# A fused attention and FFN kernel: one run of small products per head pair, and two banks each for FFN1 and attention

## The chip, the cores and the metric

One Trainium2 chip, of which the kernel uses one core. The metric is the device time of the program in microseconds. It runs once per measurement; three runs of the kernel before are shown, and a profile of one execution of it.

## The reference

Eight batches, eight heads, 576 tokens of 64 elements. Linear attention without softmax, a root-mean-square norm over each head, a low-rank mixing over the tokens (rank 32), and an FFN of 512 to 2048 to 512:

```python
kv = np.einsum('bhsd,bhse->bhde', k, v)
out = np.einsum('bhsd,bhde->bhse', q, kv)
rms = np.sqrt(np.mean(out * out, axis=-1, keepdims=True) + 1e-06)
x = (out / rms * g_norm)            # heads side by side: (batch, 576, 512)
u = x + ((x.transpose(0, 2, 1) @ U) @ V).transpose(0, 2, 1)
y = u + np.maximum(u @ w_ch1, 0.0) @ w_ch2
```

## The kernel before, in words

**The FFN.** The 4608 tokens are cut in nine blocks of 512. Each product of the FFN is made of three, with both operands split into a high and a low part: high by high, high by low, low by high. Blocks 0 to 2 (`j` in the main loop) go one by one: for each of the 16 slices `f` of the hidden width, `ffn1` (L518 to L520, 12 matmuls of 128x512 into the one bank `h`), the ReLU (`hh` on ACT in L530, `hl` on DVE in L535), and `ffn2` of the slice before (L542, 12 matmuls into four banks `y`). One slice is thus 24 matmuls of 128x512, and a quarter of it is 6. The other six blocks go two by two in three stages (`q`), by a scheme with seven products in place of eight (`first_unit` L705, `second_unit` L807, `end_unit` L757), whose combined weights are made in blocks 0 to 2, stored to DRAM and read back as `wt`. A unit of a stage is 6 matmuls of 128x512, 112 units a stage.

**Attention.** It is done by pairs (b, p): batch b, and two heads side by side in 128 columns. A pair needs these steps, and only the first three and the last use TensorE (PE), each in matmuls that are small beside those of the FFN:

- `kv`: k^T v, ten matmuls of 64 columns (L298, 20 rows in a trace, since a matmul of this type has two), copied by ACT into the diagonal 64x64 blocks of `kvb` (L175);
- `out`: q by kv. For b under 5 five matmuls of 128 columns by the block-diagonal `kvb` (four in L335, one in L337, 10 rows); for b from 5 on 20 matmuls in 64x64 quarters of the array, each head into a bank of its own (L330, 40 rows);
- the norm: for b under 5 ACT squares out of PSUM (L353, L354) and DVE multiplies out of PSUM (L391, L393); for b from 5 on ACT copies both banks out first (L346), squares in SBUF (L349), and DVE multiplies in SBUF (L389). Between them lie a sum (L374) and six small steps on DVE and ACT;
- `turn`: a transpose on DVE (L410) and five DMAs on SyncE's queue (SP) through DRAM into `ut32` (L413, L415);
- `t`: x^T U, six matmuls (four in L421, two in L424, 12 rows), then `t4`, seven small steps on ACT and DVE (L434 to L440);
- `mix`: t4 by V, one or two matmuls of up to 448 columns in two parts (L497), added by DVE to `ut32` or to the stage's input `x32` (L504), and for b up to 2 split into high and low.

**What sets the order.** In the stages PE's order is written by hand: the steps of pair p of batch b stand at `STARTS` plus `PARTS` units; the same holds in block 2 (`STARTS2`, `PARTS2`, in quarters of a slice). In blocks 0 and 1 the steps are put at half slices (`STEPS0`, `STEPS`), and a scheduler orders PE's instructions. ACT, DVE, GpSimd (POOL) and SP are ordered by the scheduler everywhere after the first 30 us; within an engine the order is kept on the chip. The first 30 us are written out (`ORDER0`).

**Banks.** PSUM has eight. In blocks 0 to 2: four for `y`, one for `h`, three that go round (`pp`) for every attention step. In the stages: two each for `z`, `x` and `y` (all called `yy` in rows), one `h` and one `big`; attention uses these last two.

Of the kernel before, what the change touches and what calls it, by code (L numbers as in the profile page):

```python
# [10 lines left out]
F32 = mybir.dt.float32  # L11
F32R = mybir.dt.float32r
# [11 lines left out]
NT = 5  # L24
# [11 lines left out]
QUAD = 5  # L36
NEARLY = 1
STEPS = dict(kv=1, out=2, t=5, mix=7, gap=5)
STEPS0 = dict(kv=6, out=7, t=11, mix=12, gap=4)
# [20 lines left out]
uvA uvD u4h vsh vsl kv0 kvb0 v4g out0 sq0 kv1 red0 ta0 hf0 rc0 kvb1 nw0 w1A out1 mul0 w1D0 kv2 sq1 w1D1 red1 w1B  # L60
tx0 kvb2 w1D2 ta1 hf1 out2 rc1 t4c0 nw1 w1H t4s0 kv3 mul1 w2A sq2 w2D0 tx1 cA red2 kvb3 w2D1 ta2 out3 lw1 lw2 lw3 hf2
# [28 lines left out]
def build(ctx: ExitStack, tc: tile.TileContext, kv_in, kvt0_in, kvt_in, q_in, uv_in, g_in, w_in, out):  # L90
# [5 lines left out]
    sc = ctx.enter_context(tc.tile_pool(name="sc", bufs=1))  # L96
    dec = ctx.enter_context(tc.tile_pool(name="dec", bufs=2))
# [4 lines left out]
    ps_p = first_y.enter_context(tc.tile_pool(name="ps_p", bufs=3, space=bass.MemoryType.PSUM))  # L102
# [10 lines left out]
    st = const.tile([P, 4, BLK], F32, name="st")  # L113
    kvb = [const.tile([P, P], F32, name=f"kvb{i}") for i in range(2)]
# [198 lines left out]
    def out_step(b, p):  # L313
        out_product(b, p)
        squares(b, p)

    def out_product(b, p):
# [16 lines left out]
        for i in range(4):
            nc.tensor.matmul(big[:, i * P:(i + 1) * P], lhsT=qt[:, TAIL + i * P:TAIL + (i + 1) * P], rhs=kb, start=True, stop=True)  # L335
# [962 lines left out]
```

## Time and profile before

| | |
|---|---|
| median of 3 runs | 850.45 us (850.35, 850.45, 852.01) |
| the profiled execution | 846.0 us, of which its span is 844.0 |
| PE busy in the span | 830.6 us, 98% |
| DVE, ACT busy | 584.4 us (69%), 435.7 us (52%) |
| granted TensorE clock, mean | 0.998 |
| DMA, mean rate over the span | 235 GB/s |

A row of the timeline has the start in us, the time in us from the first start to the last end, engine, line, operation, tiles (out<-in), the shapes and the number of instructions merged in it. Ends of matmuls are modelled, and a matmul overlaps the next, so distances here are taken from start to start. A row of waits has who waited for whom, the total in us, the number of waits and the longest. A row of windows has, for each engine, the busy time and the number of instructions, then the clock granted to PE, the busy share of the DMA engines and GB/s. A row of lines has the busy time in us, the mean of one in ns, and the idle time before them.

### The profile page before, as it was taken

What the parts mean: (1) busy time and instruction counts of PE and PEld (TensorE: products, weight loads), DVE (VectorE), ACT (ScalarE), POOL (GpSimd) and SP (SyncE); (2) the same over time, 40 slices, a digit from 0 to 9 for tenths busy, and PEclk for the clock granted to TensorE, in tenths of its full rate; (3) what the DMA queues carried; (4) which work ended last, traced back from release to release, by engine and by line L of the source; (5) the groups of instructions that cost most, each with busy time, mean ns of one, the idle gap of its engine ahead of it and who ended that gap; (6) DMA issues with size and microseconds to landing.
All of it is one profiled execution on the core that took longest, in us unless ns stands there. A gap on an engine that the chain in (4) does not pass through costs nothing.

```text
span 844.0 us, 13330 instructions
## 1 busy us (share of the span) xinstructions
PE 830.6 (98%) x4986; PEld 674.7 (80%) x4986; DVE 584.4 (69%) x1031; ACT 435.7 (52%) x795; POOL 80.8 (10%) x158
## 2 busy tenths in 40 slices
PE   7999999999999999999999999999999999999998
PEld 6778878888878787877777788777888888888887
DVE  5999975876776767567775679657836953572466
ACT  5978752433333435456645664656436724553462
POOL 2002232453400221000000000000000000000000
PEclk9999999999999999999999999999999999999999
DMA  9984765787796777366777767786555585555554
GB/s 346 415 348 139 227 222 192 236 275 241 246 291 220 266 237 271 130 239 229 257 249 266 228 237 261 239 278 234 186 200 200 178 285 189 198 197 200 200 196 153
DMA packets 66352, 198.31 MB, mean 235 GB/s; under 512 B 8176, under 2 KB 27376, under 8 KB 55536
## 3 DMA queue, kind: packets, MB, share of 16 engines
q1 hardware_dynamic: 57184, 167.97, 57.9%
q0 software_dynamic: 8960, 29.37, 10.0%
q8 instruction: 39, 0.64, 0.3%
q14 instruction: 25, 0.20, 0.1%
q10 hardware_dynamic: 144, 0.13, 0.0%
HBM read 146.84 MB, written 50.59 MB: 234 GB/s over the span
## 4 chain that ended last, share of the span: by engine, by line
PE 84%; DVE 6%; DMA 6%; ACT 2%; issue 1%; SPq 1%; POOL 0%; DVEq 0%; ACTq 0%
PE yy L705 27%; PE yy L807 25%; PE y L542 12%; PE h L518 4%; PE h L519 4%; PE h L520 4%; PE ya L757 2%; DMA raw<-w_in 1%; PE pp L335 1%; PE h L298 1%; PE pp L298 1%; DMA wd<-dec 1%; DMA w2raw<-w_in 1%; DVE dec L158 1%; PE h L330 1%
## 5 line engine op out<-in xcount | busy, mean ns | idle before, releaser
L705 PE MATMUL yy<-uc,wt 128*128 128x512 f32 x1008 | 237.0, 392 | 0.0
L705 PEld LDWEIGHTS yy<-uc,wt 128*128 128x128 f32 x1008 | 187.1, 188 | 39.7
L542 PE MATMUL y<-hh,ws 128*128 128x512 f32 x336 | 113.8, 400 | 1.7 <-ACT hh L530 1.7
L807 PE MATMUL yy<-dec,wt 128*128 128x512 f32 x468 | 114.7, 392 | 0.3 <-DVE dec L696 0.3
L807 PE MATMUL yy<-hh,wt 128*128 128x512 f32 x312 | 104.9, 393 | 0.0
L807 PEld LDWEIGHTS yy<-dec,wt 128*128 128x128 f32 x468 | 86.9, 188 | 18.9 <-DVE dec L696 0.7
L696 DVE TENSOR_TENSOR dec<-hk,dec 128x512 fp32r<-128x512 f32 x72 | 48.8, 685 | 39.5 <-ACT dec L735 39.2
L696 DVE TENSOR_TENSOR hl<-hk,hh 128x512 fp32r<-128x512 f32 x72 | 48.3, 686 | 39.6 <-ACT hh L735 39.4
L542 PEld LDWEIGHTS y<-hh,ws 128*128 128x128 f32 x336 | 61.7, 188 | 15.3 <-ACT hh L530 2.8
L807 PEld LDWEIGHTS yy<-hh,wt 128*128 128x128 f32 x312 | 58.6, 188 | 12.8
L518 PE MATMUL h<-ut,ws 128*128 128x512 f32 x168 | 67.3, 400 | 1.4 <-DVE hl L535 1.4
L519 PE MATMUL h<-ut,ws 128*128 128x512 f32 x168 | 65.6, 391 | 0.0
L542 PE MATMUL y<-hl,ws 128*128 128x512 f32 x168 | 65.6, 390 | 0.0
L520 PE MATMUL h<-ut,ws 128*128 128x512 f32 x168 | 65.5, 390 | 0.0
L807 PE MATMUL yy<-hl,wt 128*128 128x512 f32 x156 | 60.8, 390 | 0.0
L735 ACT CAST dec<-hk 128x512 fp32r<-128x512 f32 x72 | 44.2, 620 | 30.1 <-PE yy L807 14.4
L735 ACT CAST hh<-hk 128x512 fp32r<-128x512 f32 x72 | 44.2, 621 | 28.8 <-PE yy L807 24.9
L530 ACT ACTIVATE hh<-h 128x512 fp32r<-128x512 f32 x48 | 28.6, 596 | 50.7 <-PE h L520 50.5
L693 ACT COPY sp<-yy 128x1024 f32<-128x1024 f32 x35 | 35.5, 1014 | 34.5 <-PE yy L705 27.5
L535 DVE SCALAR_TENSOR_TENSOR hl<-h,hh 128x512 fp32r<-128x512 f32 x48 | 32.8, 682 | 19.6 <-ACT hh L530 19.1
L718 ACT ACTIVATE hk<-hk 128x1024 f32<-128x1024 f32 x24 | 25.4, 1060 | 33.0 <-DVE hk L717 32.8
L518 PEld LDWEIGHTS h<-ut,ws 128*128 128x128 f32 x168 | 31.5, 188 | 9.7 <-DVE hl L535 2.5
(238 smaller groups left out, 1342.2 us busy)
## 6 DMA issues: line engine op xcount, KB each, us to landing
wt<-wd SPq DMA_DIRECT2D x84, 1024.0 KB, 4.9
kv_sb<-kv_in SPq DMA_DIRECT2D x29, 512.0 KB, 5.2
raw<-w_in SPq DMA_DIRECT2D x14, 1023.6 KB, 14.8
wd<-dec POOLq DMA_DIRECT2D x44, 256.0 KB, 5.1
wd<-ws POOLq DMA_DIRECT2D x42, 256.0 KB, 4.4
q_sb<-q_in SPq DMA_DIRECT2D x29, 288.0 KB, 4.4
ut<-xd SPq DMA_DIRECT2D x28, 288.0 KB, 3.4
out<-x SPq DMA_DIRECT2D x23, 256.0 KB, 2.9
```

The lines of the kernel that those rows point to most:

```text
L518: nc.tensor.matmul(h, lhsT=w1s[f][0][:, d, :], rhs=uh[d], start=(n == 0), stop=False)
L519: nc.tensor.matmul(h, lhsT=w1s[f][0][:, d, :], rhs=ul[d], start=False, stop=False)
L520: nc.tensor.matmul(h, lhsT=w1s[f][1][:, d, :], rhs=uh[d], start=False, stop=(n == ND - 1))
L530: last["relu"] = nc.scalar.activation(out=last["hh"], in_=h, func=AF.Relu)
L535: last["low"] = nc.vector.scalar_tensor_tensor(out=hl, in0=h, scalar=0.0, in1=last["hh"].bitcast(F32), op0=ALU.max, op1=ALU.subtract)
L542: nc.tensor.matmul(acc, lhsT=w2s[f][w][:, c, :], rhs=h[:, cols], start=(f == 0 and w == 0 and h is hh), stop=(f == NF - 1 and w == 1))
L693: last["unit"] = nc.scalar.copy(out=pair_bank("P6") if name == "P1" else spare(name), in_=acc)
L696: return nc.vector.tensor_tensor(out=out, in0=a, in1=b, op=ALU.subtract)
L705: nc.tensor.matmul(acc[:, i], lhsT=w[:, ws_, e * P:(e + 1) * P], rhs=u[:, e, us], start=name in ("P1", "P5") and e == 0 and k == 0, stop=e ...
L718: last["unit"] = nc.scalar.activation(out=to, in_=to if other else acc, func=AF.Relu)
L735: last["unit"] = nc.scalar.copy(out=hh, in_=src)
L807: nc.tensor.matmul(acc[:, c], lhsT=w[:, ws_, c * P:(c + 1) * P], rhs=h, start=name in ("P1", "P5") and kk == 0 and i == 0, stop=kk == KEEP ...
```

## The change

All attention of pair `now` is gathered into `run(before, now, after)`: in one go PE does `t` of the pair before, `kv` of the pair after, and `out` of this pair. The three share two banks: `t` goes into columns 320 to 447 of the second, `kv` into the last 64 of the first (of the second for odd pairs of batch 1), the two heads of `out` into columns 0 to 319 of both. `out` is done in 64x64 quarters for all pairs, and after the first 30 us always copied out by ACT first. A table `RUNS` says where each run stands, `MIXES` where the mixes do, in quarters of a slice in the blocks and in units in the stages. In the blocks the eight banks are now: four `y`, one `h`, one `two` (FFN1 takes `h` for odd slices and `two` for even ones), two `pp`. PE's order is written by hand from the main loop on. `t4` has three buffers in place of one, `turn` follows the norm at once except for three pairs. In the first 30 us 13 matmuls of 128x128 by zeros (`wa3 wb3 wc4 wd3`) are added on PE, and a memset of `kvb` goes from DVE to POOL.

```diff
-QUAD = 5
-STEPS = dict(kv=1, out=2, t=5, mix=7, gap=5)
-STEPS0 = dict(kv=6, out=7, t=11, mix=12, gap=4)
-STARTS = {5: (0, 11, 22, 33), 6: (44, 55, 67, 78), 7: (3, 14, 25, 36)}
-PARTS2 = dict(kv=0, out=4, turn=8, t=13, mix0=17, mix1=18)
-PARTS = dict(kv=0, out=5, turn=9, t=14, mix0=19, mix1=21)
+RUNS = [((1, 0), (0, 20)), ((1, 1), (0, 28)), ((1, 2), (0, 37)), ((1, 3), (0, 45)), ((2, 0), (0, 54)),
...
+        ((6, 3), (3, 72)), ((7, 0), (3, 84)), ((7, 1), (4, 7)), ((7, 2), (4, 18)), ((7, 3), (4, 29)), (None, (4, 40))]
+MIXES = {(1, 0): ((0, 26),), (1, 1): ((0, 43),), (1, 2): ((0, 51),), (1, 3): ((0, 60),),
...
-uvA uvD u4h vsh vsl kv0 kvb0 v4g out0 sq0 kv1 red0 ta0 hf0 rc0 kvb1 nw0 w1A out1 mul0 w1D0 kv2 sq1 w1D1 red1 w1B
+uvA uvD u4h vsh vsl kv0 wa3 kvb0 v4g out0 wb3 sq0 kv1 wc4 red0 ta0 hf0 rc0 kvb1 nw0 w1A out1 mul0 w1D0 kv2 sq1 w1D1 red1 w1B
...
+def banks():
+    if "big" in second_y:
+        return ps_h.tile([P, 512], F32, name="h"), second_y["big"].tile([P, 512], F32, name="big")
+    return bank(), bank()
...
-        if b >= QUAD:
-            heads = [kv_bank_of(b), big]
-        for i in range(4):
-            nc.tensor.matmul(big[:, i * P:(i + 1) * P], lhsT=qt[:, TAIL + i * P:TAIL + (i + 1) * P], rhs=kb, start=True, stop=True)
+        for i in range(NT):
+            at = TAIL + i * P if i < 4 else 0
+            for half in (0, D):
+                for h, lo in enumerate((0, D)):
+                    nc.tensor.matmul(heads[h][half:half + D, i * D:(i + 1) * D], lhsT=qt[lo:lo + D, at + half:at + half + D],
+                                     rhs=kb[lo:lo + D, lo:lo + D], start=True, stop=True)
...
-        t4 = sc.tile([P, P], F32R, name="t4")
+        t4 = four.tile([P, P], F32R, name="t4")
...
+    def run(before, now, after):
+        one, two = banks()
+        if before:
+            t_product(*before, two[:, NT * D:NT * D + P])
+        if after:
+            kv = (two if after[0] < NATIVE and after[1] % 2 else one)[:, BLK - D:]
+            kv_product(*after, kv)
+        if now:
+            out_product(*now, (one, two))
+        if before:
+            t4_step(*before)
+        if after:
+            kv_move(*after, kv)
+            following(load_kv, *after)
+        if now:
+            squares(*now)
+            stats_step(*now)
+            mul_step(*now)
+            following(load_q, *now)
+            if now not in TURNS:
+                turn_step(*now)
...
+    rest.enter_context(tc.manual_schedule(engines={mybir.EngineType.PE}))
     for j in range(NC):
-        if j == NC - 1:
-            rest.enter_context(tc.manual_schedule(engines={mybir.EngineType.PE}))
...
-                h = ps_h.tile([P, BLK], F32, name="h")
+            h = (ps_h if f % 2 else pools["two"]).tile([P, BLK], F32, name="h")
```

How the instructions stand on three engines, at the places of which the prediction speaks. First PE in block 2, before: `out` of a pair and, elsewhere, `kv` of a pair, each alone between products of the FFN.

```order
L542 MATMUL y<-hh,w2s_515 128x512
L335 MATMUL pp<-kvb_95,q_sb 128x128 x4
L337 MATMUL pp<-kvb_95,q_sb 128x128
L518 MATMUL h<-ut,ws_579 128x512
L519 MATMUL h<-ut,ws_579 128x512
```

```order
L542 MATMUL y<-hh,w2s_536 128x512
L298 MATMUL pp<-kv_sb 64x64 x8
L298 MATMUL pp<-kvt_sb 64x64 x2
L518 MATMUL h<-ut,ws_651 128x512
L519 MATMUL h<-ut,ws_651 128x512
```

And PE in block 2 in the change, one run (L387 and L390 are `t`, L300 `kv`, L319 `out`, L508 `ffn2`):

```order
L508 MATMUL y<-hl,ws_1435 128x512
L508 MATMUL y<-hh,ws_1435 128x512
L387 MATMUL pp<-x_88,uf 32x128 x4
L390 MATMUL pp<-x_88,uf 32x64 x2
L300 MATMUL pp<-kv_sb 64x64 x8
L300 MATMUL pp<-kvt_sb 64x64 x2
L319 MATMUL pp<-kvb_100,q_sb 64x64 x20
L508 MATMUL y<-hh,ws_1435 128x512
```

What moved: the three products of three different pairs stand side by side, `out` is cut in quarters, and matmuls of the FFN follow at once. The matmuls of 128x512 are the same 3156 in both programs; the places where small ones stand between them go from 129 to 80.

Second, DVE in block 0, in the change, from the weights of slice 7 over `t4` of pair (1, 0) (L406) to the two adds of its mix (L470); L153 to L164 and L262 decode weights, L501 is `hl`:

```order
L262 TENSOR_TENSOR ws_809<-dec,ws_809 128x1024
L406 TENSOR_TENSOR t_837<-two,t_837 64x128
L158 TENSOR_SCALAR dec<-dec 128x256
L160 SCALAR_TENSOR_TENSOR dec<-dec 128x256
L501 SCALAR_TENSOR_TENSOR hl<-h,hh 128x512
L153 TENSOR_SCALAR dec<-dec 128x256
L154 TENSOR_SCALAR dec<-dec 128x1024
L164 SCALAR_TENSOR_TENSOR dec<-raw_609,top 128x1024
L158 TENSOR_SCALAR dec<-dec 128x256
L470 TENSOR_TENSOR ut_90<-pp,ut_90 128x288 x2
```

What moved: before, 13 instructions stood between the end of `t4` (L440) and the first add (L504), now 7, and the two adds, which stood apart, follow each other. PE has 12 matmuls of 128x512 between this mix and the next run, which writes the same two banks.

Third, SP's queue in block 0. Before:

```order
L200 DMA kv_sb<-kv_in 128x1024
L203 DMA kvt_sb<-kvt_in 128x256
L413 DMA xd_100<-xt 32x4x160 x2
L413 DMA xd_100<-xt 32x4x128 x2
L264 DMA wf_108<-dec 256x1x512
L415 DMA ut_87<-xd_100 128x576
L221 DMA q_sb<-q_in 128x576
```

In the change:

```order
L206 DMA kv_sb<-kv_in 128x1024
L380 DMA xd_104<-xt 32x4x160 x2
L380 DMA xd_104<-xt 32x4x128 x2
L209 DMA kvt_sb<-kvt_in 128x256
L270 DMA wf_113<-dec 256x1x512
L382 DMA ut_90<-xd_104 128x576
L227 DMA q_sb<-q_in 128x576
```

What moved: the load of k's and v's last rows (`kvt_sb`) stands behind the stores of a `turn` (`xd`), which wait for DVE's transpose; q's load stands behind `ut`, as before.

## Rows read from the trace of the kernel before

**Rows 1.** The page's first part, PE: busy us, share of the span, instructions.
```profile
PE 830.6 (98%) x4986; PEld 674.7 (80%) x4986; DVE 584.4 (69%) x1031; ACT 435.7 (52%) x795; POOL 80.8 (10%) x158
```
**Rows 2.** The waits of PE, the three longest.
```profile
PE y L542 <- ACT hh L530: 1.7, 2, 1.4
PE pp L337 <- DMA q_sb<-q_in: 1.5, 1, 1.5
PE h L518 <- DVE hl L535: 1.4, 1, 1.4
```
**Rows 3.** The chain that ended last, a stretch of stage 1 without attention.
```profile
614.38 27.22 PE yy L705 x120
```
**Rows 4.** Timeline of PE in stage 0: `kv` of a pair alone.
```profile
401.63 0.39 PE L807 MATMUL yy<-hh,wt 128*128 128x512 f32 x1
401.95 0.69 PE L298 MATMUL h<-kv_sb 128*64 128x64 f32 x16
...
402.68 0.50 PE L807 MATMUL yy<-dec,wt 128*128 128x512 f32 x1
```
**Rows 5.** The same, `t` of a pair alone.
```profile
406.67 0.39 PE L807 MATMUL yy<-hh,wt 128*128 128x512 f32 x1
406.99 0.43 PE L421 MATMUL big<-x,uf 128*32 128x128 f32 x8
...
407.44 0.50 PE L807 MATMUL yy<-hh,wt 128*128 128x512 f32 x1
407.78 0.39 PE L807 MATMUL yy<-hl,wt 128*128 128x512 f32 x1
```
**Rows 6.** The same, `out` in quarters: the first and the last of 40 rows.
```profile
408.94 1.53 PE L807 MATMUL yy<-dec,wt 128*128 128x512 f32 x6
410.40 0.27 PE L330 MATMUL h<-kvb,q_sb 64*64 64x64 f32 x1
...
410.99 0.22 PE L330 MATMUL big<-kvb,q_sb 64*64 64x64 f32 x1
411.14 1.66 PE L807 MATMUL yy<-dec,wt 128*128 128x512 f32 x6
```
**Rows 7.** Timeline of PE in block 0: `out` in matmuls of 128 columns.
```profile
64.41 0.39 PE L542 MATMUL y<-hh,ws 128*128 128x512 f32 x1
64.63 1.05 PE L335 MATMUL pp<-kvb,q_sb 128*128 128x128 f32 x8
...
65.66 0.71 PE L542 MATMUL y<-hh,ws 128*128 128x512 f32 x2
```
**Rows 8.** Timeline of PE in block 1: `t` of one pair and `kv` of another side by side.
```profile
173.66 0.39 PE L542 MATMUL y<-hh,ws 128*128 128x512 f32 x1
173.98 0.43 PE L421 MATMUL pp<-x,uf 128*32 128x128 f32 x8
...
174.44 0.69 PE L298 MATMUL pp<-kv_sb 128*64 128x64 f32 x16
174.95 0.29 PE L298 MATMUL pp<-kvt_sb 128*64 128x64 f32 x4
175.17 0.50 PE L518 MATMUL h<-ut,ws 128*128 128x512 f32 x1
175.50 0.39 PE L519 MATMUL h<-ut,ws 128*128 128x512 f32 x1
```
**Rows 9.** Windows: most of block 0, and the slow stretch of the first 30 us.
```profile
36.00:104.00 68.00, 68.00 (x392) 55.45 (x391) 63.20 (x121) 52.85 (x81) 11.24 (x16) 1.00 0.71 253
11.00:16.00 5.00, 4.99 (x41) 4.37 (x42) 4.16 (x13) 3.02 (x9) 0.11 (x1) 0.66 1.04 408
```
**Rows 10.** Timeline of PE and of DVE: one part of a mix, and its add.
```profile
109.20 0.29 PE L497 MATMUL pp<-v,t 128*128 128x288 f32 x1
113.50 0.44 DVE L504 TENSOR_TENSOR ut<-pp,ut 128x288 f32<-128x288 f32 x1
```
**Rows 11.** Lines of ACT: the square of a pair of b from 5 on.
```profile
L349 ACT ACTIVATE xt<-x 128x640 f32<-128x640 f32 x12 | 8.9, 741 | 0.4
```

More of the change, by code (lines that the diff above doesn't have):

```diff
@@ L495, in mix_part @@
         lo, hi = ((0, m), (m, S))[part]
-        mp = big_bank(b)[:, 0:hi - lo]
+        mp = (bank() if "big" not in second_y else ps_h.tile([P, 512], F32, name="h") if part else second_y["big"].tile([P, 512], F32, name="big"))[:, 0:hi - lo]
         nc.tensor.matmul(mp, lhsT=state[b, p]["t4"], rhs=v4[:, lo:hi], start=True, stop=True)
@@ L851, in build @@
         nc.gpsimd.memset(t[TAIL:P, 4, :], 0.0)
-    nc.gpsimd.memset(kvb[1], 0.0)
+    for t in kvb:
+        nc.gpsimd.memset(t, 0.0)
     make_identity(nc, ident)
@@ L1085, in build @@
     ahead = FIRST + 1
-    def prep_schedule(b):
-        todo = {}
-        if b == 2:
-            todo[1] = [lambda: [split_cols(1, p, 1, nc.vector) for p in range(NPAIR)]]
-        steps = STEPS0 if b == 1 else STEPS
-        for p in range(NPAIR):
-            own = pair_steps(b, p)
-            for at in ("t",) if (b, p) == (1, 0) else ("kv", "out", "turn", "t"):
-                todo.setdefault(steps["gap"] * p + steps["out" if at == "turn" else at], []).append(own[at])
-            todo.setdefault(steps["gap"] * p + steps["mix"], []).append(lambda p=p: mix_step(b, p))
-        for pair, (now, _) in EARLY.items() if b == 2 else ():
-            for at, n in now.items():
-                todo.setdefault(n, []).append(pair_steps(*pair)[at])
-        return todo
@@ L1125, in build, with following @@
+    def following(load, b, p):
+        b, p = (b, p + 1) if p + 1 < NPAIR else (b + 1, 0)
+        if b < B:
+            load(b, p)
+    first_p.close()
+    for name, n in (("p", 2), ("two", 1)):
+        pools[name] = first_y.enter_context(tc.tile_pool(name=f"ps_{name}2", bufs=n, space=bass.MemoryType.PSUM))
     later = {}
@@ L1136, in build @@
                          for i, t in enumerate(x32_tiles(0))])
-    for (b, p), (_, at) in EARLY.items():
-        for name in at:
-            if name != "mix":
-                at_block(at[name], pair_steps(b, p)[name])
-        at_block(at["mix"], lambda b=b, p=p: mix_step(b, p))
-    for (b, p), start in STARTS2.items():
-        for at, what in pair_steps(b, p).items():
-            at_block(start + PARTS2[at], what)
-    for e, pair in enumerate((2, 3)):
-        at = STARTS2[4, pair] + PARTS2["mix1"] + 1
-        at_block(at, lambda e=e: factor(0, "P1 P5 P6 P4 P2 P7 P3", slice(e, e + 1)))
@@ L1148, in build @@
-    for b, starts in STARTS.items():
-        for p, start in enumerate(starts):
-            for at, what in pair_steps(b, p).items():
-                at_stage((b - 5) // 2, start + PARTS[at], what)
-    for b, at in CARRY.items():
+    pairs = [pair for pair, _ in RUNS]
+    at(RUNS[0][1], lambda: run((1, 0), None, (1, 1)))
+    for i, (pair, spot) in enumerate(RUNS[1:], 1):
+        at(spot, lambda i=i, pair=pair: run(pairs[i - 1] if i > 1 else None, pair, pairs[i + 1] if i + 2 < len(pairs) else None))
@@ new lines, in build @@
+    for pair, spot in TURNS.items():
+        at(spot, lambda pair=pair: turn_step(*pair))
+    for pair, spots in MIXES.items():
+        if pair[0] > 2:
+            for part, spot in enumerate(spots):
+                at(spot, lambda pair=pair, part=part: mix_part(*pair, part))
+        else:
+            at(spots[0], lambda pair=pair: mix_step(*pair))
+    for e, pair in enumerate((2, 3)):
+        at_block(MIXES[4, pair][1][1] + 1, lambda e=e: factor(0, "P1 P5 P6 P4 P2 P7 P3", slice(e, e + 1)))
```

195 lines of the change are left out of this document (71 added, 124 removed), and 9 rows, old and new, of tables (MIXES, RUNS).

## The prediction

> **What bounds the kernel now.** First the page's engines: PE is busy 830.6 of 844.0 us [rows 1]. Then its waits: the three longest, all in blocks 0 to 2, come to 4.6 us [rows 2], so neither DVE nor a DMA sets the time there, but PE's own work. Where only products of 128x512 run, 120 of them take 27.22 us, 0.227 each [rows 3]; 3156 of them would be 716 us. The first of them starts at about 30 us. So some 90 us are left for small products and waits, and the change works on these. Busy time doesn't tell what a small product costs, because it overlaps its neighbours. I read the timeline instead, from the start of the last 128x512 before it to the starts of the first two behind it, less 0.227 a step.
>
> **What a piece costs.** Alone in a stage:
> - `kv`: 402.68 less 401.63, less 0.227, is 0.82 [rows 4]. The first 128x512 behind a small piece holds the next one back: 0.34 from start to start instead of 0.227 [rows 5]. That is 0.11 more: 0.93.
> - `t`: 407.44 less 406.67, less 0.227, plus the 0.11: 0.65 [rows 5].
> - `out` in quarters: 411.14 less 408.94, less 6 x 0.227, is 0.84; plus 0.11: 0.95 [rows 6].
> - `out` by 128 columns: 65.66 less 64.41, less 0.227, is 1.02. The two behind it are merged in a row of 0.71 us, where two undisturbed ones would take 0.39 + 0.227 = 0.62, so 0.09 is held back: 1.11 [rows 7].
>
> **What a join saves.** One place before the change has `t` and `kv` of different pairs side by side: 175.17 less 173.66, less 0.227, is 1.28, plus 0.33 less 0.227 behind it: 1.38 [rows 8]. Apart they are 1.58, so the join saves 0.20. A join of `kv` and quartered `out` is in no row. Its bounds: 0, if the switch between two small forms costs what a switch to 128x512 and back does, and 0.20 as above. I take 0.20, since it too joins two forms that both use part of the array.
>
> **The sum on PE.** A run of three costs 0.65 + 0.93 + 0.95 - 2 x 0.20 = 2.13.
> - Before, behind the first FFN product: 28 `t`, 27 `kv`, 16 `out` by 128 columns, 12 quartered: 28 x 0.65 + 27 x 0.93 + 16 x 1.11 + 12 x 0.95 = 72.5 us.
> - After: 25 full runs, 53.3; the five incomplete places (`out` alone, `t`+`kv`, `kv`+`out`, `t`+`out`, `t`) 0.95 + 1.38 + 1.68 + 1.40 + 0.65 = 6.1. Together 59.4, so 13.1 less.
> - Some pieces before are cut in two or interleaved by the scheduler, two whole joins stand there already; I take 0.4 more for the difference. **13.5 us off PE.** With the 27 joins that end in `out` at nothing it is 8.1.
>
> The mixes keep their products and are left out.
>
> **Copies.** In blocks each pair gets one more pass on ACT, a square in SBUF of 0.74 us [rows 11], and its two copies take the place of two squares. ACT is busy 52.85 of 68 us even in block 0 [rows 9], so 15 x 0.74 lie beside PE's work. If that cover goes, a ReLU comes late, and `ffn2` waits as it does before the change (1.7 us in two waits). DVE's multiply is the same work in one instruction.
>
> **Waits.** The second bank for FFN1 takes away what L518 waited for: `h` need not be read by `hl` before the next slice starts. I count that 1.4 as gone, and q's 1.5 too, since every q is now loaded one whole run ahead [rows 2]. The 1.7 of `hh` I leave. A new wait: in block 0 the run at quarter 28 follows the mix of (1, 0) by 12 products, 2.7 us. Its banks come free when DVE has added both parts. Before the change an add ended up to 113.94 - 109.20 = 4.7 us behind its product [rows 10]; it may be at once, so the wait is 0 to 2.0. In the change's order seven other instructions of DVE stand ahead of these adds, five of them decoding, and DVE is busy 63.20 of 68 us there [rows 9], which speaks for the long end. There are three such places; I take 2.6 in all. Eight more mixes stand 18 products, 4.1 us, ahead of a run: 0 to 0.6 each, taken as 0. So 2.9 go and 2.6 come.
>
> **The first 30 us.** The products by zeros stand where PE waits for loads and copies. From 11 to 16 us PE had a granted clock of 0.66, so part of it at the lower level of 1.2 GHz, after waits; at the full clock the same 4.99 us would take 3.3 [rows 9]. That bounds the gain at 1.7. The DMA engines are busy throughout (1.04) with the weights that DVE needs, so I take 0, and the cover is the loads. The memset moves beside idle time.
>
> **Sum:** -13.5 - 2.9 + 2.6 = -13.8 us. The profiled execution goes from 846.0 to 832.2. The median of the runs is 4.45 above the profiled one, and I keep that distance: 850.45 - 13.8 = 836.65, **836.5 us**.
>
> **A page against the quarters.** The 40 rows of `out` start within 410.40 to 410.99, 0.015 us apart [rows 6]; the 16 rows of `kv` start in 0.51, 0.032 apart [rows 8]. The Trainium skill (TensorE: Matmul & The Clock Gate, section "Wait — 56ns, not 53.3ns?") says that matmuls never start closer than about 25 ns however few columns they have. By that page 40 rows would take 1.0 us, 0.4 more, and 16 pairs 6.5 us: some 843. The rows here, where four quarters of the array work side by side, speak against it; rival 1 is the nearest to it that rows give.
>
> **Rivals.**
> 1. *Quarters at kv's pace.* If in the blocks the rows of `out` follow each other at the 0.032 of `kv`, 40 take 1.28 instead of 0.59: 16 x 0.69 = 11 back, 847.5. For it: no trace has quarters in the blocks. Against: the same instructions in the stages [rows 6]. Chance 0.02.
> 2. *Block 0 gives it back.* There four `t`, five `kv` and four `out` go from 11.7 to 9.5 us, so PE gains 2.2 in 68. DVE then has its 63.2 in 65.8, 96%, and its decoding feeds PE. If DVE can't be pressed, block 0 stays as long as it was, and ReLUs and adds come late for another 2.5: 841.2. For it: the DVE share. Against: PE is busy all 68 us there before the change [rows 9], so DVE kept ahead. Chance 0.16.
> 3. *All waits go.* The 4.6 and the new ones vanish, and the start gives 1.5: 850.45 - 13.5 - 4.6 - 1.5 = 830.9. For it: two banks for `h`, and every step placed by hand. Chance 0.14.
> 4. *Joins that end in `out` save nothing:* 27 x 0.20 back, 841.9. For it: no row has one. Against: the other join [rows 8]. Chance 0.08.
> 5. *Slower: two banks hold PE.* Each run writes both attention banks, PE keeps its order, so everything behind waits for DVE's adds and ACT's copies. With a hold of H us from a mix's product to its second add, the three near places wait H - 2.7 and the eight others H - 4.1; with the 2.6 counted already, this eats the gain of 13.8 from a mean H of 5.2 us on. At 5.7 us it is 3 x 3.0 + 8 x 1.6 - 2.6 = 19.2 more, 855.9. The longest hold found is 4.7 [rows 10], so it takes a DVE that falls behind throughout, not in block 0 alone. Chance 0.04. The Trainium skill names this trap (TensorEngine Tiling (Array Packing), section "PSUM Bottleneck"): packing speeds up TensorE but not the emptying of PSUM, whose copy may become the bottleneck. The trace shows no such wait in the stages, where two banks already serve attention.
> 6. *It isn't what it says.* The order shows the runs side by side on PE, so only an effect of nothing is left, if the FFN's products grew longer: 850.5, chance 0.01.
>
> **How the numbers follow.** The forecast has 0.55, its own range 833.5 to 839.5 (new waits of 0 to 5.5). The whole range takes in rival 3 below and rivals 2 and 4 above: 830.0 to 843.0, which leaves out rivals 1, 5 and 6 and the tails, under 2 in 10. A measurement of this kernel tells 0.2%, 1.7 us, from no change. Faster by more: all but rivals 5 and 6 and a remainder, 0.94; within: 0.02; slower: 0.04.
>
> **What would show it.** A run in the timeline of PE: 2.1 us from its last 128x512 to the second behind it, less two steps, in blocks and stages alike. If `kv` to `out` takes more than 0.15 from the last start to the first, rival 4. Waits of PE: `t` or `kv` (L387, L300) on DVE's add (L470) are rivals 2 and 5; on `kv_sb`, `kvt_sb` or `q_sb` they are the loads behind `xd` in SP's queue, which I price at nothing. Weights (`ws`) late for L484: rival 2. The prediction is wrong if a run costs over 2.5, or if waits after 30 us come to over 9 us.

## The result, and the profile after

The change takes 836.43 us by the median of four runs (835.28 to 837.33), against 850.4 before: a ratio of 0.9838, 95% interval 0.981 to 0.9867. 836.5 was forecast. The profiled execution took 837.33 us with a span of 835.6. The second profile of each kernel is among the experiments; where the text says "both profiles", it means these.

The page after, the first part's line (it answers to [rows 1]):

```profile
PE 820.7 (98%) x5492; PEld 673.2 (81%) x5492; DVE 585.4 (70%) x1016; ACT 443.4 (53%) x810; POOL 80.3 (10%) x159
```

PE is still busy 98% of the span, in 9.9 us less. A run of three in block 1, timeline of PE (start, us, engine, line, operation):

```profile
177.39 0.39 PE L486 MATMUL h<-ut,ws 128*128 128x512 f32 x1
177.71 0.43 PE L387 MATMUL pp<-x,uf 128*32 128x128 f32 x8
...
178.16 0.69 PE L300 MATMUL pp<-kv_sb 128*64 128x64 f32 x16
...
178.90 0.81 PE L319 MATMUL pp<-kvb,q_sb 64*64 64x64 f32 x40
179.64 0.50 PE L484 MATMUL h<-ut,ws 128*128 128x512 f32 x1
179.98 0.40 PE L485 MATMUL h<-ut,ws 128*128 128x512 f32 x1
```

By the prediction's rule: 179.64 less 177.39, less 0.227, is 2.02; 0.34 less 0.227 behind it is 0.11; together 2.13. That is the median of all 25 full runs, in blocks and stages alike. The 40 rows of `out` lie within 178.90 to 179.64, under 0.02 us apart on average, so also in the blocks the 25 ns of the Trainium skill (TensorE: Matmul & The Clock Gate, "Wait — 56ns, not 53.3ns?") don't hold for them; the measurement decides.

The waits of PE after (waited for: us in total, times, longest), which answer to [rows 2]:

```profile
PE pp L463 <- DVE t L406: 4.8, 2, 3.4
PE pp L387 <- DVE x L363: 1.2, 1, 1.2
...
PE yy L671 <- ACT t L405: 0.9, 1, 0.9
PE pp L300 <- DVE ut L470: 0.8, 1, 0.8
```

The three waits of before are gone. In their place mixes wait for `t4`, a run for the multiply of the pair before, and one run for an add. Windows after (PE, PEld, DVE, ACT, POOL busy, granted clock, DMA share, GB/s); the first two answer to [rows 9]:

```profile
36.00:104.00 68.00, 62.61 (x412) 50.55 (x411) 61.52 (x115) 53.86 (x79) 9.98 (x16) 0.98 0.70 251
11.00:16.00 5.00, 4.76 (x52) 4.08 (x50) 4.40 (x15) 3.57 (x10) 0.29 (x1) 1.00 1.05 407
102.60:107.00 4.40, 4.40 (x11) 3.42 (x11) 4.25 (x10) 2.74 (x4) 1.35 (x2) 0.50 0.87 292
```

Behind the longest wait the granted clock is 0.50, the lower level of 1.2 GHz:

```profile
97.97 0.39 PE L508 MATMUL y<-hh,ws 128*128 128x512 f32 x1
101.78 0.82 PE L463 MATMUL pp<-v,t 128*128 128x288 f32 x2 [3.42 <-DVE t L406]
102.39 0.63 PE L484 MATMUL h<-ut,ws 128*128 128x512 f32 x1
102.82 0.63 PE L485 MATMUL h<-ut,ws 128*128 128x512 f32 x1
```

The products of 128x512 start 0.43 us apart here instead of 0.227; eleven or twelve of them cost another 2.3 us.

**Where the time went.** The starts of the first FFN product of block 0 (30.44 after, 30.40 before), of block 1 (138.58, 132.26) and of the first product of the stages (345.49, 347.88) cut both spans in four. Both profiles of each kernel, with what PE's attention work changes there by the prediction's prices:

| us | before | after | difference of the means | by the prices of the pieces |
|---|---|---|---|---|
| first 30 us | 30.4, 31.1 | 30.4, 30.7 | -0.2 | 0 |
| block 0 | 101.9, 101.7 | 108.1, 107.6 | +6.0 | -0.4 |
| blocks 1 and 2 | 215.6, 218.6 | 206.9, 207.5 | -9.9 | -5.8 |
| stages and end | 496.2, 496.1 | 490.1, 490.0 | -6.1 | -7.0 |

So block 0 became 6 us longer, and the rest more than paid for it. The cut before block 1 isn't at quite the same work: 376 products of 128x512 lie between the cuts of block 0 before and 372 after, and the four, 0.9 us, lie in block 1 now. On equal work block 0 lost 7 us, and blocks 1 and 2 gained 10.8.

### The profile page after: what moved, and what is told of

The parts are those of the page before. It is cut to its first block, busy times and chain, and to the rows that moved or that the text cites. A ratio compares the mean times of both kernels' runs of the same rounds, so it can differ in the third digit from the quotient of the medians.

```text
span 835.6 us, 14368 instructions
## 1 busy us (share of the span) xinstructions
PE 820.7 (98%) x5492; PEld 673.2 (81%) x5492; DVE 585.4 (70%) x1016; ACT 443.4 (53%) x810; POOL 80.3 (10%) x159
## 4 chain that ended last, share of the span: by engine, by line
PE 83%; DVE 6%; DMA 6%; ACT 3%; issue 1%; SPq 0%; ACTq 0%; DVEq 0%
PE yy L671 25%; PE yy L773 23%; PE y L508 13%; PE h L484 5%; PE h L485 5%; PE h L486 4%; DMA w1raw<-w_in 2%; PE ya L723 2%; DMA out<-x 1%; DMA raw<-w_in 1%; PE pp L300 1%; PE pp L319 1%; DVE dec L164 1%; PE h L300 1%; DVE uc L575 1%
## 5 line engine op out<-in xcount | busy, mean ns | idle before, releaser
L671 PE MATMUL yy<-uc,wt 128*128 128x512 f32 x1008 | 234.1, 391 | 0.9 <-ACT t L405 0.9
L508 PE MATMUL y<-hh,ws 128*128 128x512 f32 x336 | 113.4, 393 | 0.0
L508 PEld LDWEIGHTS y<-hh,ws 128*128 128x128 f32 x336 | 63.1, 188 | 13.8
L773 PEld LDWEIGHTS yy<-hh,wt 128*128 128x128 f32 x312 | 58.6, 188 | 12.4
L484 PE MATMUL h<-ut,ws 128*128 128x512 f32 x168 | 67.5, 402 | 0.0
L485 PE MATMUL h<-ut,ws 128*128 128x512 f32 x168 | 66.6, 396 | 0.0
L486 PE MATMUL h<-ut,ws 128*128 128x512 f32 x168 | 66.4, 395 | 0.0
L508 PE MATMUL y<-hl,ws 128*128 128x512 f32 x168 | 65.8, 391 | 0.0
L773 PE MATMUL yy<-hl,wt 128*128 128x512 f32 x156 | 60.7, 389 | 0.0
L659 ACT COPY yy<-yy 128x1024 f32<-128x1024 f32 x17 | 17.0, 998 | 43.4 <-PE yy L671 40.5
L501 DVE SCALAR_TENSOR_TENSOR hl<-h,hh 128x512 fp32r<-128x512 f32 x48 | 32.7, 682 | 9.4 <-ACT hh L496 9.4
```

Source lines behind the costliest of these rows:

```text
L484: nc.tensor.matmul(h, lhsT=w1s[f][0][:, d, :], rhs=uh[d], start=(n == 0), stop=False)
L485: nc.tensor.matmul(h, lhsT=w1s[f][0][:, d, :], rhs=ul[d], start=False, stop=False)
L486: nc.tensor.matmul(h, lhsT=w1s[f][1][:, d, :], rhs=uh[d], start=False, stop=(n == ND - 1))
L501: last["low"] = nc.vector.scalar_tensor_tensor(out=hl, in0=h, scalar=0.0, in1=last["hh"].bitcast(F32), op0=ALU.max, op1=ALU.subtract)
L508: nc.tensor.matmul(acc, lhsT=w2s[f][w][:, c, :], rhs=h[:, cols], start=(f == 0 and w == 0 and h is hh), stop=(f == NF - 1 and w == 1))
L659: last["unit"] = nc.scalar.copy(out=pair_bank("P6") if name == "P1" else spare(name), in_=acc)
```

## The experiments

The medians below are of one chip per comparison, with the kernel before run between them (its medians there: 849.42 in 1 to 3, 849.05 in 4 and 8 to 10, 847.59 in 5 to 7, 848.40 in 11). Ratios are to that. "Above the change" is above the 837.1 of experiment 1.

**1. Both kernels again.** No edit. 

> The kernel before, unchanged, with a second profile. Theory A (the first profile of before, 846.0, lay 4.4 below its own median because waits vary between executions): span and waits of PE differ by several us from the first profile, while a 128x512 product keeps its 0.227 us. Theory B (the distance is fixed, something outside the span): the profile comes out at 846 again and the median at 850.4.

> The change, unchanged, with a second profile. If waits vary between executions (theory A), the 3.4 us wait of the mix of pair (1, 1) and the 5 us at a granted clock of 0.50 behind it are absent or smaller, the waits on t4 come to under 5 us in place of 6.2, and the median stays at 835.3 to 837.4. Theory B: wait and clock drop come again, with 3.4 us within 0.3.

Before: 848.05 us by ten runs (845.73 to 853.43), its profiled run 849.55. After: 837.1 by six (835.7 to 839.67), ratio 0.9858 (0.9828 to 0.9888), profiled run 837.53. Theory A holds: the first profile of before was a short execution. Its second has 3.2 us of waits on `hh` (1.7 in the first) and 2.1 on q (1.5). In the second profile of after the mix of (1, 1) waits 2.2 in place of 3.4, as A said, but the runs wait 2.9 for the multiply in place of 1.2, and the lower clock came again, for nine products. The waits move; behind the first 30 us they sum to 8.5 and 8.0 us.

**2. Two buffers for the turned pair.**

```diff
+    turned = ctx.enter_context(tc.tile_pool(name="turned", bufs=2))
...
-            xt = s["xt"] = sc.tile([P, 4, NT, 32], F32, name="xt")
+            xt = s["xt"] = turned.tile([P, 4, NT, 32], F32, name="xt")
...
```

> Two buffers in place of one for the turned and the squared pair. Theory 1 (the mix of pair (1, 1) waits because ACT, in order, stands at the square until the transposed pair before has gone out of that buffer): the wait of 3.4 us and the drop of the granted clock go, 832 to 834.5 us by the median, 2 to 4 us less than the change. Rival (t4 is late because DVE and ACT have more to do than fits before the mix): t4 stays late, the waits on it stay over 4 us, the median within 1 us of the change.

Why this buffer: ACT of the change ahead of the long wait (the bracket is ACT's idle time before the row and what ended it):

```profile
90.92 1.11 ACT L167 COPY dec<-raw 128x1024 uint8<-128x1024 uint8 x1 [2.05 <-DMA wf<-dec]
...
95.01 0.44 ACT L329 ACTIVATE x<-pp 128x320 f32<-128x320 f32 x1
97.15 0.74 ACT L333 ACTIVATE xt<-x 128x640 f32<-128x640 f32 x1 [1.71 <-issue]
...
99.92 0.28 ACT L405 CAST t<-two 64x128 fp32r<-64x128 f32 x1
```

The square waits until the pair before has left the buffer, and `t4`'s cast is queued behind it. With two buffers:

```profile
95.10 0.74 ACT L334 ACTIVATE xt<-x 128x640 f32<-128x640 f32 x1
...
97.90 0.28 ACT L406 CAST t<-two 64x128 fp32r<-64x128 f32 x1
```

The square comes 2.05 us earlier and the mix starts at 99.75 instead of 101.78. About 0.4 of both was there before this place (ACT's copy of x in the row above starts at 94.63 here, 95.01 in the change); the rest is the wait of 1.71 that is gone. The mix still waits 1.9, the lower clock comes again, and the runs now wait 3.2 us for the multiply. 836.41 us, ratio 0.9847 (0.9822 to 0.9873), 0.7 under the change on that chip: the mechanism is there, the time goes to the rival.

**3. Mixes of batch 1 later.**

```diff
-MIXES = {(1, 0): ((0, 26),), (1, 1): ((0, 43),), (1, 2): ((0, 51),), (1, 3): ((0, 60),),
+MIXES = {(1, 0): ((0, 29),), (1, 1): ((0, 47),), (1, 2): ((0, 53),), (1, 3): ((0, 62),),
```

> The four mixes of batch 1 stand two to four quarter slices later, (1, 1) now behind the run at quarter 45. Both theories of the late t4: its waits of 3.4 and 1.4 us in block 0 go, 2 to 5 us less than the change. Rival (block 0 is bound by DVE, so a wait that is moved comes back elsewhere, at the ReLU, the run behind the mix or the weights): new waits in block 0 of the same sum, the median within 1 us of the change; the runs at 45 and 54 then wait for the adds of the mixes before them.

836.28 us, ratio 0.9843 (0.9818 to 0.9869). The rival: the mixes now wait 3.6 us for ACT's copy of x, a run 3.2 for the multiply. Block 0 takes 107.3. The scheduler also put ACT's and DVE's instructions of block 0 in another order here, as it did in experiments 4, 5 and 8 to 10; in 2 and 7 that order is the change's, in 6 and 11 nearly so.

**4. Some of the decoding on POOL.**

```diff
-            nc.vector.tensor_tensor(out=w[:, 1], in0=t, in1=w[:, 0].bitcast(F32), op=ALU.subtract)
+            (nc.gpsimd if f % 2 else nc.vector).tensor_tensor(out=w[:, 1], in0=t, in1=w[:, 0].bitcast(F32), op=ALU.subtract)
```

> The change with every second low half of the decoded weights (128x1024, 1.22 us each on DVE) on POOL, which is busy 2.5 us of 10 in block 0. Theory (the waits of PE in block 0, on t4 and on the multiply, come because DVE and ACT are pressed there by the decoding): five of these passes, 6.1 us, leave DVE between 56 and 126 us, and the waits there fall from about 7 us to under 3: 832 to 834. Rival (they are the length of the chain through ACT and DVE, transposed store and load, not the load of DVE): within 1 us of the change. Second rival: POOL's pass is longer by so much that the weights come late, 1 us or more above the change.

842.22 us, ratio 0.9918 (0.9896 to 0.994): the second rival by the time, though PE waits only 1.0 us for these weights. POOL's pass takes 2.4 us, and DVE's pass over the raw weights is stretched where the two meet (the lines' groups: ns min/median/max, first and last start):

```profile
L262 POOL TENSOR_TENSOR ws<-dec,ws x7: 2382/2397/2841, 46.7 to 128.5; 128x1024 fp32r<-128x1024 f32 x7
```
```profile
L164 DVE SCALAR_TENSOR_TENSOR dec<-raw,top x14: 1214/1224/3302, 37.0 to 125.1; 128x1024 uint32<-128x1024 uint32 x14
```

So this run adds time of its own and can't say what DVE's load does. The next one can.

**5. Less decoding on DVE.** The later chunks go without the clamp of their exponents, a part of the computation that this kernel leaves out.

```diff
         def clamp():
-            nc.vector.tensor_scalar(out=c, in0=b, scalar1=0x7f7f7f7f, scalar2=None, op0=ALU.bitwise_and)
+            if n == DM:
+                nc.vector.tensor_scalar(out=c, in0=b, scalar1=0x7f7f7f7f, scalar2=None, op0=ALU.bitwise_and)
...
-            nc.vector.tensor_scalar(out=c, in0=c, scalar1=3, scalar2=0x38383838,
+            nc.vector.tensor_scalar(out=c, in0=c if n == DM else b, scalar1=3, scalar2=0x38383838,
```

> The change without the clamp of the weights' exponents in the later chunks: two DVE passes fewer per chunk (0.29 and 0.71 us, ten chunks between 56 and 126 us, some 10 us in all); that part of the computation is left out. Theory (DVE is pressed by the decoding in block 0, and PE's waits there come from it): the waits of 7 to 8 us in block 0 fall to under 3, block 0 ends 4 to 6 us earlier, 831 to 833 by the median. Rival (the length of the chain from a run through the copies, the multiply, the transposed store and load and t4's seven steps to the mix sets them, wherever DVE stands): waits of 5 us or more stay, the median over 834.5.

Windows of the change, then of this kernel:

```profile
56.00:126.00 70.00, 63.21 (x533) 50.18 (x532) 59.56 (x108) 49.30 (x77) 13.30 (x23) 0.95 0.60 189
```
```profile
56.00:126.00 70.00, 62.57 (x472) 49.76 (x470) 51.72 (x87) 49.45 (x76) 13.24 (x22) 0.93 0.59 191
```

DVE is busy 7.8 us less, and PE waits as long as before; its two longest kinds are

```profile
PE pp L464 <- DVE t L407: 4.5, 2, 4.2
PE pp L301 <- DVE ut L471: 2.9, 1, 2.9
```

837.58 us, ratio 0.9876 (0.9856 to 0.9896). The theory's waits under 3 us and its 831 to 833 didn't come. But the rival isn't shown by that, since these are other waits: the run at quarter 28 stands 2.9 us at the adds of the mix before it (0.8 in the change), one mix 4.2, and behind that no step is late. With less decoding the steps from `out` to the multiply did become shorter (table below). So DVE's load may be a part of it; taking some off saved no time in the order that the scheduler made of the rest.

**6. `t4` with fewer changes of engine.**

```diff
-            nc.scalar.copy(out=other[R * i:R * (i + 1)], in_=two[R * (1 - i):R * (2 - i)])
+            nc.vector.tensor_copy(out=other[R * i:R * (i + 1)], in_=two[R * (1 - i):R * (2 - i)])
...
-        nc.scalar.copy(out=t4[0:2 * R], in_=two)
+        nc.vector.tensor_copy(out=t4[0:2 * R], in_=two)
```

> The change with three of the four ACT steps of t4 (two copies by 32 rows of 0.30 us, one cast of 0.29) on DVE, so that the chain changes engine once in place of six times; DVE gets some 0.85 us more per pair, ACT as much less. Theory (the mixes wait because each change of engine queues t4 behind passes of 0.7 to 1.2 us): the waits on t4 of 2.2 to 4.8 us in block 0 and of 0.9 in the stages go, 833 to 835 by the median. Rival (DVE's load sets the waits): 0 to 3 us more than the change, the waits on the multiply grow.

835.1 us, ratio 0.9854 (0.9832 to 0.9876), not to be told from the change. Its profile has block 0 at 105.9, some 2 us less; the waits on `t4` there are 2.2, on the multiply 2.9. Neither forecast was met: inconclusive.

**7. Without the products by zeros.**

```diff
-uvA uvD u4h vsh vsl kv0 wa3 kvb0 v4g out0 wb3 sq0 kv1 wc4 red0 ta0 hf0 rc0 kvb1 nw0 w1A out1 mul0 w1D0 kv2 sq1 w1D1 red1 w1B
+uvA uvD u4h vsh vsl kv0 kvb0 v4g out0 sq0 kv1 red0 ta0 hf0 rc0 kvb1 nw0 w1A out1 mul0 w1D0 kv2 sq1 w1D1 red1 w1B
...
```

> The change without the twelve products by zeros in the first 30 us. Theory (they stand beside the loads and the decoding that bound the start): the first FFN product starts at 30 to 31 us as before, the median within 0.8 us of the change, and the granted clock between 11 and 16 us is lower than with them. Rival (they keep the clock up and so shorten the start): 1 to 1.7 us more.

All thirteen are gone. 834.83 us, ratio 0.9851 (0.9832 to 0.9871). The first FFN product starts at 30.1, and the window is again what it was before the change:

```profile
11.00:16.00 5.00, 5.00 (x41) 4.42 (x42) 3.97 (x12) 2.88 (x9) 0.22 (x1) 0.66 1.05 415
```

The products keep the granted clock at 1.00 there, and it buys nothing: the theory holds.

**8. One bank for the FFN's first product.**

```diff
-            h = (ps_h if f % 2 else pools["two"]).tile([P, BLK], F32, name="h")
+            h = ps_h.tile([P, BLK], F32, name="h")
```

> The change with one bank for the FFN's first product in the blocks, as before it. Theory (the second bank took away the waits on hl, 1.4 us in the profile of before): 1 to 3 us more than the change, and a wait of the FFN's first product on hl of 1 us or more is back. Rival (the second bank bought nothing, because block 0 is paced by DVE and ACT together, so PE only waits in another place): within 1 us of the change, the waits of PE in block 0 again 7 to 9 us in sum. Third: several us more in blocks 1 and 2 too, where now every hl must end before the next slice.

846.65 us, ratio 0.9986 (0.9968 to 1.0003), some 10 us above the change. The first line of PE's waits:

```profile
PE h L484 <- DVE hl L501: 11.0, 8, 2.6
```

The four longest, 2.0 to 2.6 us, stand behind 78.8, 118.4, 290.8 and 331.4 us, so in blocks 0 and 2: the theory's sign, the third case's size. Without the second bank the rest of the change would gain next to nothing.

**9. The runs taken apart.**

```diff
-    def run(before, now, after):
+    def run(before, now, after, parts="tko"):
...
-        at(spot, lambda i=i, pair=pair: run(pairs[i - 1] if i > 1 else None, pair, pairs[i + 1] if i + 2 < len(pairs) else None))
+        for part, n in zip("tko", (-1, 0, 1)):
+            at((spot[0], spot[1] + n), lambda i=i, pair=pair, part=part: run(pairs[i - 1] if i > 1 else None, pair, pairs[i + 1] if i + 2 < len(pairs) else None, part))
```

> The change with every run of three taken apart: the product with x^T one quarter slice earlier, kv at the spot, out one quarter slice later, in the same two banks; the first run, which has no out, stays whole. Theory (a join saves 0.20 us on PE, and each of 52 joins is given up): 10.4 us more on PE, 846 to 848 by the median. In the timeline each of the three pieces then costs what it costs alone, 0.65, 0.93 and 0.95. Rival (a join saves nothing where it ends in out, as rival 4 of the prediction has it): 5.2 us more, 841 to 843. Second rival (the two banks, now held a quarter slice longer on either side, stop PE): over 850, with waits of t or kv on the adds.

847.09 us, ratio 0.998 (0.9963 to 0.9998): 10.0 above the change, 10.4 expected. The pieces cost 0.657, 0.942 and 0.941 by the median, 2.54 in place of 2.13; `out` in block 1, for one (183.91 - 182.85 - 0.227 + 0.11 = 0.94):

```profile
182.85 0.39 PE L486 MATMUL h<-ut,ws 128*128 128x512 f32 x1
183.16 0.81 PE L319 MATMUL pp<-kvb,q_sb 64*64 64x64 f32 x40
183.91 0.50 PE L508 MATMUL y<-hh,ws 128*128 128x512 f32 x1
184.24 0.39 PE L508 MATMUL y<-hl,ws 128*128 128x512 f32 x1
```

**10. `out` by 128 columns in the blocks.**

```diff
+        if "two" in pools and "big" not in second_y:
+            big, small = heads[0], heads[1][:, 0:P]
+            for i in range(4):
+                nc.tensor.matmul(big[:, i * P:(i + 1) * P], lhsT=qt[:, TAIL + i * P:TAIL + (i + 1) * P], rhs=kb, start=True, stop=True)
+            nc.tensor.matmul(small, lhsT=qt[:, 0:P], rhs=kb, start=True, stop=True)
...
```

> The change with out of the blocks by 128 columns as before it (15 pairs; the stages keep the quarters), in the same runs and banks. Theory (quarters cost 0.95 alone, full columns 1.11, and the join with kv is lost, 0.20): 15 x 0.36 = 5.4 us more, 841 to 843. Rival (the join saves whatever follows): 15 x 0.16 = 2.4 more, 838.5 to 840. Second rival (quarters are no cheaper in the blocks): within 1 us.

842.88 us, ratio 0.9934 (0.9914 to 0.9955), 5.8 above the change. A run in the blocks costs 2.504 by the median of 15, 0.37 more than in quarters, and 15 x 0.37 = 5.6. The theory holds with its 0.36: the join of `kv` with 128 columns saves nothing, that with quarters saves 0.20.

**11. Edits 2 and 6 together.**

> Two edits together: two buffers for the turned pair, and the three ACT steps of t4 on DVE. Theory (PE's waits in block 0 are the length of the chains through the queues of ACT and DVE, in order, with a stall of ACT on the one buffer and changes of engine in t4): with both, t4 of pair (1, 1) is there 3 us or more earlier after its product than in the change, the waits on t4 in block 0 fall under 1 us, block 0 takes 104 to 105.5 us instead of 107.6 to 108.1, and the ratio to before is 0.980 to 0.984. Rival (what one wait gives is taken by the next, above all by the multiply before the next run): block 0 takes 106 us or more, the waits on the multiply of 2.9 us stay or grow, the ratio over 0.984.

837.87 us, ratio 0.9869 (0.9839 to 0.9899), block 0 109.6: the rival. The mix of (1, 1) starts at 98.30 without a wait, 3.5 us earlier, as the theory said, and no wait on `t4` is left in block 0. But the next run waits 7.0 us for the multiply. ACT, DVE and SP's queue of this kernel show why:

```profile
98.02 0.58 ACT L497 ACTIVATE hh<-h 128x512 fp32r<-128x512 f32 x1
103.09 1.09 ACT L168 COPY dec<-raw 128x1024 uint8<-128x1024 uint8 x1 [4.49 <-DMA wf<-dec]
```
```profile
100.00 0.16 DVE L344 TENSOR_TENSOR ta<-r,half 128x10 f32<-128x10 f32 x1
...
104.21 0.29 DVE L154 TENSOR_SCALAR dec<-dec 128x256 uint32<-128x256 uint32 x1 [3.32 <-ACT dec L168]
104.42 0.16 DVE L345 TENSOR_TENSOR ta<-ta,r 128x10 f32<-128x10 f32 x1
...
107.78 0.82 DVE L364 TENSOR_TENSOR x<-x,half 128x640 f32<-128x640 f32 x1
```
```profile
96.99 0.33 SPq L383 DMA_DIRECT2D ut<-xd  x1
97.75 2.21 SPq L271 DMA_DIRECT2D wf<-dec  x2
```

Read from below: the store of a decoded chunk is issued at 97.75, right behind the load of `ut`, which stands in the same queue until the transposed pair has landed in DRAM. ACT can't start the next chunk until that store has freed the buffer, and stands 4.49 us. DVE's next decoding pass waits for ACT, and the second step of Newton's iteration (L345), ready since 100.2, is queued behind it. So the multiply ends at 108.6, and the run waits.

So one chain stands behind a step of another, in three queues that each keep their order. To give `wf` a queue or a third buffer of its own wasn't tried.

**What all of them share.** In the change the pairs (1, 1) to (1, 3) of block 0 are tied to each other: `out`, copies, square, multiply, `t`, `t4`, mix, and the next pair's `out` in the same run as the `t` of this one. From the first row of `out` of (1, 1) to the mix of (1, 3) it is 124.33 - 64.63 before ([rows 7] has the start) and 134.20 - 73.44 after. The end before, then two rows of after:

```profile
124.33 0.42 PE L497 MATMUL pp<-v,t 128*128 128x288 f32 x2
```
```profile
73.44 0.28 PE L319 MATMUL pp<-kvb,q_sb 64*64 64x64 f32 x2
...
134.20 0.42 PE L463 MATMUL pp<-v,t 128*128 128x288 f32 x2
```

| us | stretch begins | ends | length | block 1 begins |
|---|---|---|---|---|
| before, both profiles | 64.6, 65.3 | 124.3, 124.9 | 59.7, 59.6 | 132.3, 132.8 |
| after, both profiles | 73.4, 73.7 | 134.2, 133.8 | 60.8, 60.1 | 138.6, 138.2 |
| 2, two buffers | 73.0 | 133.0 | 60.0 | 137.4 |
| 5, less decoding | 75.5 | 135.8 | 60.3 | 140.1 |
| 6, `t4` on DVE | 73.2 | 132.0 | 58.8 | 136.4 |
| 7, no zeros | 73.1 | 132.9 | 59.8 | 137.3 |
| 11, edits 2 and 6 | 73.4 | 135.9 | 62.5 | 140.2 |

The stretch takes 60 us before and after, within 3, but that isn't a length that the steps need. Before, PE waited for none of them: the next `out` stood 5 us behind `t`, and a mix was issued 3 to 5 us after its `t4` was ready. In experiment 5 x was ready 1.7, 3.7 and 6.7 us ahead of its run, and the length is the same. The change's table of spots gives the stretch 32 quarter slices, 32 x 6 x 0.227 = 43.6 us, with three runs and two mixes some 50.5; the other 10 are waits of PE and what the clock costs behind them. What changed is how long the steps take, first of `out` to the end of the multiply, then of `t` to the end of `t4`:

| us, pairs (1, 1), (1, 2), (1, 3) | `out` to multiply | `t` to `t4` |
|---|---|---|
| before | 12.2, 12.2, 10.0 | 6.2, 7.4, 8.5 |
| before, second profile | 12.3, 11.9, 9.8 | 6.1, 7.3, 8.5 |
| after | 14.4, 18.0, 12.3 | 13.7, 11.7, 6.2 |
| after, second profile | 14.4, 18.1, 11.5 | 12.4, 11.3, 6.2 |
| 2, two buffers | 14.4, 17.9, 11.5 | 12.1, 11.3, 6.2 |
| 5, less decoding | 13.2, 15.5, 6.9 | 14.5, 6.2, 6.2 |
| 9, runs taken apart | 10.0, 13.6, 9.2 | 9.3, 7.9, 3.8 |
| 11, edits 2 and 6 | 14.4, 19.6, 10.8 | 10.2, 9.8, 4.2 |

Rows of PE and DVE for `t` and `t4` of (1, 1) and for `out` and the multiply of (1, 2), before and then after (the `out` of after follows in the run of this `t`, at 89.05):

```profile
78.85 0.42 PE L421 MATMUL pp<-x,uf 128*32 128x128 f32 x8
...
83.97 1.05 PE L335 MATMUL pp<-kvb,q_sb 128*128 128x128 f32 x8
...
84.72 0.28 DVE L440 TENSOR_TENSOR t<-two,t 64x128 fp32r<-64x128 f32 x1
...
95.88 0.27 DVE L393 TENSOR_TENSOR x<-pp,half 64x128 f32<-64x128 f32 x1
```
```profile
87.97 0.42 PE L387 MATMUL pp<-x,uf 128*32 128x128 f32 x8 [1.17 <-DVE x L363]
...
101.34 0.28 DVE L406 TENSOR_TENSOR t<-two,t 64x128 fp32r<-64x128 f32 x1
...
106.27 0.82 DVE L363 TENSOR_TENSOR x<-x,half 128x640 f32<-128x640 f32 x1
```

These lengths give the waits. From a `t` to its mix, six quarter slices later, the spots leave 10.3 us (134.20 - 123.94 for the last pair, which waits for nothing). The `t4` of (1, 1) and (1, 2) take 13.7 and 11.7, and PE waits 3.4 and 1.4. With the 6.2 to 8.5 of before it wouldn't have waited.

Why they take longer: in the change a pair's `t` and the next pair's `out` reach ACT and DVE together. The cast of `t4` (99.92 in experiment 2's first rows) stands behind both copies and the square of the next pair. Before, `t4` was done at 85.00, and that pair's squares began at 85.06. Experiment 9 separates the three products by a quarter slice each, and on ACT the cast of this `t4` stands ahead of the copies again:

```profile
87.07 0.43 PE L387 MATMUL pp<-x,uf 128*32 128x128 f32 x8
```
```profile
95.59 0.29 ACT L405 CAST t<-two 64x128 fp32r<-64x128 f32 x1
95.91 0.77 ACT L329 ACTIVATE x<-pp 128x320 f32<-128x320 f32 x2
```

Its steps sum to 32.8 and 21.0 us, against 44.7 and 31.6 in the change and 34.4 and 22.1 before, with the same work on ACT and DVE as the change. (Its longest wait, 4.2 us for a multiply, comes from spots that leave two quarter slices less between `out` and `t`.) So by this run the join that saves PE 10 us also makes the steps behind it longer. How the lengthening divides among the order of the queues, the decoding and the stalls on stores isn't settled, since the scheduler ordered ACT and DVE anew there.

Block 0's 6 us then come out of waits and clock. In the first profiles PE waits 7.3 us there against 1.9 before, the lower clock costs some 2.3, PE's work is 0.4 less and four products, 0.9, lie outside the cut: 6.4, measured 6.2. Whether spots with more room between `t` and its mix, or with `t4` ahead of the copies, would win this back wasn't tried and stays open.

## Why the prediction was right, and where it was not

- **PE's work: right.** t, kv, quartered `out` and the run were priced at 0.65, 0.93, 0.95 and 2.13; they measured 0.657, 0.94, 0.94 and 2.13 (experiment 9). `t` + `out` came out at 1.40 as forecast, `t` + `kv` at 1.54 in place of 1.38, since a `kv` of batch 1, with its last rows in quarters, costs 1.07 alone (58.38 - 57.19 - 0.227 + 0.11, in block 0 of before). All small products of attention without their waits come to about 60.7 us, 59.4 forecast; by the same reading those of before come to 74.3, so 13.6 are gone, 13.5 forecast. The open join of `kv` and quartered `out`, between 0 and 0.20, is 0.20: rival 4 falls, and with the 0.94 of `out` in the blocks rival 1 too.
- **The second bank: right sign, wrong reason for its size.** The 1.4 us of `hl` went. But the bank is worth 10 us in the changed kernel (experiment 8). The sum asked only what the wait cost before, and not what it would have become.
- **q's wait: gone, as forecast.** Together with `hl` and, in the second profile, `hh` it gave blocks 1 and 2 2.9 to 5.3 us beyond PE's work, which is why they fell by 8.7 to 11.1 (on equal work 0.9 more, which stays unexplained).
- **The new waits: wrong place, and 3 to 4 times the size.** "There are three such places; I take 2.6 in all" is the step that failed. The bank wait was found exactly at the run at quarter 28, 0.8 us, and nowhere else: rival 5 falls, and with it the trap that the Trainium skill (TensorEngine Tiling (Array Packing), section "PSUM Bottleneck") names. What came was not in the sum: `t4` late for its mix and x late for its run, 5 to 6 us in block 0, 0.9 in the stages, and some 2 us at the lower clock behind them. The sum asked only when banks come free and took the steps on ACT and DVE behind a run to last as long as before. They lasted longer: `t` to `t4` up to 13.7 us where the spots leave 10.3 and the trace of before had 6.2 to 8.5.
- **Rival 2 in part.** Block 0 did give back, 6 us, more than the 4.7 that rival took. But PE's work there fell by 0.4 and not by 2.2: one `out` and one `kv` of the four and five stood in block 1 or later before (`out` of (2, 0) at 136.81) and stand in block 0 now. And full DVE alone isn't it: with 7.8 us less work there PE waited as long, at other places (experiment 5).
- **Copies on ACT: right** that no ReLU came late: no wait on `hh` is among those after. But the copies and the square, taken to lie beside PE's work at no price, are among the rows that `t4` stood behind (experiment 2).
- **The first 30 us: right** at 0 (experiment 7).
- **The number.** From profile to profile the sum said -13.8; it is -8.7 by the first pair (846.0 to 837.33) and -12.0 by the second (849.55 to 837.53). By the medians it is -14.0 and, in experiment 1, -12.3. The profile of before was a short execution, so the distance of 4.45 between the median and it, "and I keep that distance", was no property of the kernel. It stood in part for waits that the first profile hadn't shown and that the change also removes, and made up for the waits that the sum had missed. The prediction's own sign of being wrong, waits of over 9 us behind the first 30, was missed by little: 8.5 and 8.0, without the clock's 2. 836.5 was right by PE's work, and by two errors in the waits that cancel; that they cancel to 0.1 us is luck.

## What to carry to other kernels

Where PE is the bound, price small products by the starts of the large ones around them; such prices held to 0.01 us, in joins too. But a join on PE also sends the steps behind its products to the other engines at one moment, and there they queue. So set the room that a table of spots gives each step (10.3 us from `t` to its mix here) against the length that the step will have in the new order of the queues, and not in the trace of before. A single step made faster then moves the wait to the next step. And take a second profile of the kernel before, when a sum of waits is to be set against a median.

## What the runs showed of the hardware that was not expected

- A wait of PE can cost more than itself. Behind waits of 1.7 to 7.0 us the granted clock often fell to the lower level (0.50 in 102.6 to 107 after a wait of 3.42, eleven or twelve products at 0.43 instead of 0.227 us), though not each time: behind one of 3.19 in experiment 3 and one of 2.95 in experiment 7 it stayed at 1.00, as it did behind the waits of up to 2.1 us in the two profiles of before.
- While POOL ran its subtraction in experiment 4, some passes of DVE became longer: L164 took 2.27, 2.28, 2.31 and 3.30 us where it overlapped POOL's subtraction by 1.19, 1.20, 1.23 and 2.21 us, and 1.22 elsewhere, so about the overlap is added. Not only passes over two tensors did: L158, over one tensor of 128x256, took 1.16 and 2.44 us instead of 0.29. DVE's transpose (0.84), a pass over one tensor of bytes (L154, 0.69) and `hl` (L501, 0.65), which reads one of its tensors from PSUM, kept their times.
- The products by zeros kept the granted clock at 1.00 in 11 to 16 us (0.66 without), with no effect on the time that the runs can tell.
